# A decayed-attention and hard-swish MLP kernel: the first half tile's units given out more slowly, and the last tile's output units put in a row

## The chip, the cores and the metric

The kernel runs on one core of a Trainium2 chip. The metric is the device time of one execution in microseconds (us). The kernel before was run three times: 1083.11, 1084.06 and 1090.14 us, median 1084.06 us. One further execution was profiled; it is the one that the views below show.

## The reference

There are 8 batches of 8 heads with 576 rows of 64 elements, all in f32. The attention is causal, with a decay between a query and a key that is the difference of a running sum of log f. The result goes, with the heads of a row side by side, through a two-layer MLP.

```python
def _attn_ref(q, k, v, f):                     # (8, 8, 576, 64), f: (8, 8, 576)
    scores = np.matmul(q, k.transpose(0, 1, 3, 2)) / np.sqrt(D)
    cum = np.cumsum(np.log(np.clip(f, 0.0001, 1.0)), axis=-1)
    scores = np.where(causal, -1000000000.0, scores + cum[..., :, None] - cum[..., None, :])
    attn = np.exp(scores - np.max(scores, axis=-1, keepdims=True))
    attn = attn / (np.sum(attn, axis=-1, keepdims=True) + 1e-09)
    return np.matmul(attn, v)
def _moe_ref(x, w_in, w_out):                  # x (4608, 512), w_in (512, 2048), w_out (2048, 512)
    h = x @ w_in
    g = h * np.clip(h + 3.0, 0.0, 6.0) / 6.0
    return g @ w_out
```

## The kernel before, in words

**Numbers in two parts.** A product of f32 numbers is computed as three fp16 matmuls (high by high, high by low, low by high), or as one fp32r matmul plus one for the remainders. This is why each line of a product stands three times in the MLP (L781, L782, L783 and L834, L835, L836) and why the scores have a second matmul (L609 and L612). The weights arrive in a wide format, and are decoded and split while attention already runs; `w_step` gives that work out piece by piece, and DVE's share of the split is L295.

**The steps.** The outer loop (L974 to L1042) runs over the list `VH` (L97): four steps of kind A (the first 256 query rows of batch 0, two heads at a time), eight of kind B (the other rows of batch 0's heads) and 56 of kind F, a full head each, of batches 1 to 7. The steps are numbered 0 to 67. Step 12 is the first head of the second batch, step 13 its second head. Names such as `pn_13_0` hold the step and the half of the head.

**One full head.** SP loads q and k into `ST` (L412) and the decay rows into TK and TQ (L418, L420). POOL copies q and k into TQ and TK (L447, L448). SP copies these by DMA to the other half of the partitions, into T7 and T1 (L454, L455), and POOL subtracts to get the remainders (L456, L459). PE then computes the scores `pn` in two halves (L609, L612); DVE adds the mask and takes the row maxima (`pp`, L620; `nb`, L626), ACT takes the exponential (L632), ACT, DVE and POOL write the two fp16 parts into a `ring` buffer (L646, L649, L655), SP transposes each half by DMA into `pT` (L667, two transposes a head), and PE multiplies by v into `pav` (L692 to L697). After each second head, the pair's rows are normalised (L721 to L733) and transposed by SP into `xT` and `xS` (L748, L753), which are the MLP's input. There are three buffers each of TK, TQ and ST, two of T1 and T7, three rings. v of a batch is loaded into `vst` (L360, L361) and its largest element found by DVE (L366) and PE (`pt_v`, L184), for the scale of its fp16 parts.

**The MLP as units.** A tile is 512 rows of a batch; the 64 rows left over are done for two batches at a time (`moe_short`). `h_unit` computes 128 of the 2048 hidden columns for a tile: 12 matmuls into one bank, then ACT (L789), DVE (L792, tile `r`), ACT (L793) and DVE (L794) write the two parts of `gT`. `out_unit` computes the output of 128 rows: 48 matmuls into one bank `po`, an ACT copy into `o` (L840, pool of two buffers) and an output DMA. Batch 0's tile is two half tiles of 256 rows: the first can begin when the four A steps are done, the second when the B steps are. Both kinds take their banks from `mm_tile`: two banks of one pool in turn, and, where `three` is set, each third tile another bank. The first half tile has `three=False` throughout and so the two banks alone.

**When the units come.** They stand in a queue, and `fill(1)`, called eight times in a step, adds `rates[0]` to a credit and issues units while the credit is at least 1 (L941 to L951). An h unit of the half tile costs 1.05 credits, an output unit 7.6. `rates[0]` is set once a step (L991), from `F_RATE[0]` in all of batch 0, from `F_RATE[1]` in the second batch, and after that so that what is left is spread evenly over the heads. The first half tile enters the queue at step 5, as 16 h units and 2 output units, some 32 credits. The second half tile enters at step 13.

**What sets the order.** The calls above give a priority; the order of instructions on each engine is then written out when the program is built, by a scheduler that has a model of the durations. On the chip each engine runs its list in order. `behind(on)` (L762) tells the scheduler that an instruction is to be issued after the last one on the list `chain`. In the kernel before this holds for the h units of the last tile (batch 7) and of the last leftover rows; its four output units and the two half-width ones of the leftover rows (`po_3456_0`, `po_3456_256`) are free in their order.

Of the kernel before, what the change touches and what calls it, by code (L numbers as in the profile page):

```python
# [20 lines left out]
def kernel(  # L21
# [10 lines left out]
    nc = tc.nc  # L32
# [3 lines left out]
    B = vS.shape[0]  # L36
# [9 lines left out]
    NFC = DFF // P  # L46
# [35 lines left out]
    NQK, NL, NST = 3, 2, 3  # L82
    W_RATE = (8, 2, 4)
    H_COST = 1.05
    F_RATE = (0.6, 0.45)
    PIN = 0
    PIN0 = 1
    LOW_W = 0
# [45 lines left out]
    w2 = cpool.tile([P, NFC + AHEAD, 2, DM], F16, name="w2")  # L134
# [18 lines left out]
    SV, IV, UO, UX, A1 = 0, 8, 16, 24, 32  # L153
# [47 lines left out]
    def scol(c):  # L201
        return SC[:, c:c + 1]
# [339 lines left out]
    def scores(v):  # L542

        i, j = v % NQK, v % NL
        ph = p2.tile([P, 1600], F32, tag="PHL", name=f"pf_{v}")

        def group(dst, k0, q0, q1, m):
            ks = slice(k0, k0 + P)
            nc.tensor.matmul(dst, TK[i][0:97, ks], TQ[i][0:97, q0:q1], start=True, stop=False)
            nc.tensor.matmul(dst, T1[j][:, ks], T7[j][:, q0:q1], start=False, stop=(m == 0))  # L550
            if m:
                nc.tensor.matmul(
                    dst[:, 0:m], W[:m, 4 * P:], ident16[:m, :m], start=False, stop=True
                )

        pc = 0
        for parts_, exps in pieces(v):
            ps = ps_s.tile([P, 2, 512], F32, tag="S", name=f"ps_{v}_{pc}")
            for bk, o, k0, q0, w, m in parts_:
                group(ps[:, bk, o:o + w], k0, q0, q0 + w, m)  # L560
            for e, (o, w, nb) in enumerate(exps):
                dst = ph[:, o:o + w]
                if nb == 2:
                    src = ps[:, :, :w // 2]
                    dst = dst.rearrange("p (a b) -> p a b", a=2)
                else:
                    src = ps.rearrange("p a b -> p (a b)")[:, e * 512:e * 512 + w]
                nc.scalar.activation(dst, src, AF.Exp, bias=bias_p, scale=0.125)
                pc += 1
            yield  # L570
            yield ph
# [7 lines left out]
    for half in NAT:  # L579
        g = [0]  # L580
# [179 lines left out]
    chain = []  # L760

    def behind(on):  # L762
        return tc.issue_after(chain[-1]) if on and chain else nullcontext()

    def mm_tile(name, three):

        turn[0] += 1
        if three and turn[0] % 3 == 0:
            return ps_t.tile([P, TT], F32, tag="tr", name=name)
        return ps_m.tile([P, TT], F32, tag="mm", name=name)  # L770
# [56 lines left out]

    def out_unit(s, three, col, rows_, gs=None, cols=(0, DM)):
        g = gT if gs is None else gs
        c = slice(*cols)  # L830
        po = mm_tile(f"po_{rows_[0]}_{cols[0]}", three)[:, c]
        ts_ = slice(s * P, (s + 1) * P)
        for fc in range(NFC):
            nc.tensor.matmul(po, g[:, 0, fc, ts_], w2[:, fc, 0, c], start=(fc == 0), stop=False)  # L834
            nc.tensor.matmul(po, g[:, 0, fc, ts_], w2[:, fc, 1, c], start=False, stop=False)  # L835
            nc.tensor.matmul(po, g[:, 1, fc, ts_], w2[:, fc, 0, c], start=False, stop=(fc == NFC - 1))  # L836
            if fc % 2 and fc < NFC - 1:
                yield 2.0 - H_COST
        o = p2.tile([P, DM], F32, tag="o", name=f"o_{rows_[0]}_{cols[0]}")
        nc.scalar.activation(o[:, c], po, AF.Copy, scale=scol(col))  # L840
        w = P // len(rows_)
        for i, r0 in enumerate(rows_):
            nc.sync.dma_start(out[r0:r0 + w, c], o[i * w:(i + 1) * w, c])
        yield 2.0 - H_COST

    def moe_tile(t, c0=0, c1=TT):
        last = t == B - 1
        if last:
            gs = vst.bitcast(F16).rearrange("p c e -> p (c e)")[:, 0:2 * NFC * P]
            gs = gs.rearrange("p (a f t) -> p a f t", a=2, f=NFC)  # L850
        for fc in range(NFC):
            j, new = divmod(fc, NFC // NG)
            if new == 0 and c0 == 0:
                while j not in w_in_done:
                    next(w_in_q, None)
                moe_scale_in(t, j)
            yield from h_unit(t, fc, c0, c1)
            if last and new == 1:
                yield from h_short(t // 2, j, gs)
        if t == 0:  # L860
            for _ in wq:
                pass
        if c0 == 0:
            moe_scale_out(t)
        r0 = t * S + (64 if t else 0)
        for s in range(c0 // P, c1 // P):
            yield from out_unit(s, t > 0 or s * P >= QA, UO + t, [r0 + s * P])
        if last:
            for cols in ((0, DM // 2), (DM // 2, DM)):
                yield from out_unit(0, True, UX + t, [(t - 1) * S, t * S], gs, cols)  # L870

    def moe_short(u):
        for j in range(NG):
            yield from h_short(u, j, gT)
        a, b = 2 * u, 2 * u + 1
        yield from out_unit(0, True, UX + b, [b * S - 64] if a == 0 else [a * S, b * S])
# [55 lines left out]
    def even(h):  # L932

        heads = (1 - h) % H + 1
        return min(max((left[0] - RESERVE) / (8 * heads), 0.5), 1.25)
# [38 lines left out]
    for i, (kind, n) in enumerate(VH):  # L974
# [13 lines left out]
        if moved is not None:  # L988
            done(moved)
            moved = None  # L990
        rates[0] = F_RATE[0] if kind == "B" else F_RATE[b] if b < 2 else even(h)  # L991
        sg = rows(i) if kind == "F" else scores(i)
# [95 lines left out]
```

## Time and profile before

| | |
|---|---|
| median of three runs | 1084.06 us (1083.11 to 1090.14) |
| the profiled execution's own time | 1081.36 us |
| span in the profile | 1079.5 us |
| granted TensorE clock, mean | 0.983 |
| busy share of PE, DVE, ACT, POOL | 94%, 66%, 54%, 38% |
| PE busy between 310 and 1050 us | 736.79 of 740 us |
| PE busy between 130 and 310 us | 156.91 of 180 us |

PE is TensorE's matmuls, PEld its weight loads, DVE VectorE, ACT ScalarE, POOL GpSimd, SP SyncE, which issues the DMAs. The span counts from the first to the last recorded instruction; the profiled execution's own time is 1.86 us longer than its span and 2.7 us under the median of the three runs. Times in the views are us from the start of the span. In a row of a timeline, the numbers ahead are the start and the time of one instruction or of a group, and what stands in brackets at the end is how long the engine had been idle and what ended that. "issue" means that the profile shows nothing that was waited for.

### The profile page before, as it was taken

How to read it: one execution, taken by the hardware profiler on the slowest of the kernel's cores; microseconds unless marked ns; L12 is line 12 of the kernel's file. 1: busy time of each engine (PE TensorE's matmuls, PEld its weight loads, DVE VectorE, ACT ScalarE, POOL GpSimd, SP SyncE). 2: the span in 40 equal slices, each digit the busy share in tenths (PEclk: the TensorE clock that was granted, in tenths of full speed). 3: DMA queues.
4: the chain of work that ended last, by engine and by line, in shares of the span. 5: the costliest groups of instructions: out<-in, count | busy, mean ns of one | idle time of the engine just before them, and what ended most of it. 6: DMA issues, size and time to landing. Idle time of an engine off the chain costs nothing.

```text
span 1079.5 us, 21234 instructions
## 1 busy us (share of the span) xinstructions
PE 1016.3 (94%) x7698; PEld 608.5 (56%) x7698; DVE 714.6 (66%) x1903; ACT 587.5 (54%) x1190; POOL 407.8 (38%) x505
## 2 busy tenths in 40 slices
PE   2889987899989999999999999999999999999997
PEld 1557846765545665555555755555555755545545
DVE  6887968776986669865875668766865678505400
ACT  4787736664664456744654457555654566415400
POOL 7344434546534444543343345444434442100000
PEclk9989988989999999999999999999999999999999
DMA  8976326877767586577645666666565555400001
GB/s 250 287 215 198 111 60 127 147 173 161 147 139 149 118 160 119 115 141 143 145 90 123 127 150 132 128 136 162 99 118 124 96 108 87 91 30 1 1 3 47
DMA packets 259300, 133.79 MB, mean 124 GB/s; under 512 B 226964, under 2 KB 228812, under 8 KB 259196
## 3 DMA queue, kind: packets, MB, share of 16 engines
q1 hardware_dynamic: 259196, 132.44, 55.8%
q8 instruction: 61, 1.00, 0.4%
q14 instruction: 43, 0.35, 0.1%
HBM read 47.93 MB, written 9.73 MB: 53 GB/s over the span
## 4 chain that ended last, share of the span: by engine, by line
PE 66%; DVE 12%; issue 6%; DMA 6%; ACT 5%; POOL 3%; SPq 1%; ACTq 0%; POOLq 0%; DVEq 0%
PE po L834 10%; PE po L836 10%; PE po L835 10%; PE ph L781 7%; PE ph L783 6%; PE ph L782 6%; PE pn L609 3%; PE pn L612 3%; DMA vst<-in_vS_dram 2%; DVE pp L620 2%; ACT pp L632 2%; PE pav L703 2%; PE low L287 1%; DMA pT<-ring 1%; DVE gT L794 1%
## 5 line engine op out<-in xcount | busy, mean ns | idle before, releaser
L632 ACT ACTIVATE pp<-pp,nb 128x192 f32<-128x192 f32 x280 | 138.4, 552 | 148.8 <-DVE nb L626 143.7
L834 PE MATMUL po<-w,gT 128*128 128x512 f16 x560 | 210.2, 383 | 6.1 <-DVE r L792 4.7
L836 PE MATMUL po<-w,gT 128*128 128x512 f16 x560 | 209.7, 382 | 0.0
L835 PE MATMUL po<-w,gT 128*128 128x512 f16 x560 | 209.5, 382 | 0.0
L781 PE MATMUL ph<-xT,w 128*128 128x512 f16 (+1 forms) x576 | 201.8, 359 | 6.2 <-DVE r L792 6.2
L782 PE MATMUL ph<-xT,w 128*128 128x512 f16 (+1 forms) x576 | 200.9, 358 | 0.0
L783 PE MATMUL ph<-xT,w 128*128 128x512 f16 (+1 forms) x576 | 200.8, 358 | 0.0
L649 DVE TENSOR_TENSOR ring<-pp,ring 128x128 f16<-128x128 f32 (+2 forms) x216 | 138.9, 652 | 85.8 <-ACT ring L646 85.0
L620 DVE CUSTOM_DVE_ANT_0 pp<-pn,W 128x192 f32<-128x192 f32 x280 | 123.1, 481 | 34.9 <-PE pn L612 23.8
L447 POOL TENSOR_SCALAR TK<-ST 64x576 fp32r<-64x576 f32 (+1 forms) x68 | 50.8, 747 | 247.2 <-PE pn L609 172.5
L459 POOL TENSOR_TENSOR T<-ST,T 64x576 fp32r<-64x576 f32 (+1 forms) x68 | 101.4, 1492 | 88.8 <-DMA T<-TK 83.9
L609 PE MATMUL pn<-TK,TQ 68*128 68x192 f32 x336 | 125.5, 387 | 6.6 <-issue 5.5
L793 ACT CAST gT<-r 128x512 f16<-128x512 f32 (+1 forms) x144 | 81.7, 568 | 77.6 <-DVE r L792 77.3
L792 DVE SCALAR_TENSOR_TENSOR r<-r,ph 128x512 f32<-128x512 f32 (+1 forms) x144 | 88.9, 619 | 51.1 <-ACT r L789 50.7
L612 PE MATMUL pn<-T,T 128*128 128x192 f32 x336 | 114.6, 368 | 2.2 <-POOL T L459 2.2
L794 DVE TENSOR_TENSOR gT<-r,gT 128x512 f16<-128x512 f32 (+1 forms) x144 | 102.2, 714 | 19.4 <-ACT gT L793 18.2
L789 ACT ACTIVATE r<-ph,bias_r,SC 128x512 f32<-128x512 f32 (+1 forms) x144 | 103.9, 725 | 19.2 <-PE ph L783 14.1
L646 ACT CAST ring<-pp 128x192 f16<-128x192 f32 x280 | 113.8, 450 | 0.0
L456 POOL TENSOR_TENSOR T<-ST,TQ 64x576 fp32r<-64x576 f32 (+2 forms) x68 | 99.2, 1459 | 15.5 <-PE pn L612 5.8
L836 PEld LDWEIGHTS <-gT 128*128 128x128 f16 x560 | 55.0, 99 | 67.5 <-issue 7.4
L835 PEld LDWEIGHTS <-gT 128*128 128x128 f16 x560 | 55.0, 99 | 67.3 <-issue 11.3
L840 ACT ACTIVATE o<-po,SC 128x512 f32<-128x512 f32 (+1 forms) x37 | 24.7, 673 | 120.7 <-PE po L836 115.8
(154 smaller groups left out, 2026.4 us busy)
## 6 DMA issues: line engine op xcount, KB each, us to landing
ST<-in_qk_dram SPq DMA_DIRECT2D x64, 288.0 KB
T<-TK SPq DMA_DIRECT2D x64, 144.0 KB
out_dram<-o SPq DMA_DIRECT2D x33, 256.0 KB
ring<-in_w_out_dram SPq DMA_DIRECT2D x16, 512.0 KB
T<-TQ SPq DMA_DIRECT2D x56, 144.0 KB
vst<-in_vS_dram SPq DMA_DIRECT2D x7, 1040.0 KB
ring<-in_w_in_dram SPq DMA_DIRECT2D x9, 512.0 KB
w<-in_w_in_dram SPq DMA_DIRECT2D x7, 512.0 KB
```

The lines of the kernel that those rows point to most:

```text
L609: nc.tensor.matmul(dst, TQ[i][0:D + 4, qs], TK[i][0:D + 4, a:e], start=True, stop=False)
L612: nc.tensor.matmul(dst, T7[j][:, qs], T1[j][:, a:e], start=False, stop=True)
L620: nc.vector.tensor_tensor_reduce(pp[:r, w:w + kw], pn[:r, o:o + kw], W[:r, 4 * P + r - kw:4 * P + r], 1.0, -3.0e38, ALU.add, ALU.max, accu ...
L632: nc.scalar.activation(x_, x_, AF.Exp, bias=nb[:r, e0 + x:e0 + x + 1], scale=0.125)
L646: nc.scalar.copy(hl[:r, h0[c]:h0[c] + kw], pp[:r, at[c]:at[c] + kw])
L649: eng.tensor_tensor(hl[:r, a:a + c * P], pp[:r, at[c] + 64:at[c] + kw], hl[:r, h0[c] + 64:h0[c] + kw], op=ALU.subtract,)
L781: nc.tensor.matmul(ph, w1[0][:, cc, fs_], xh, start=(cc == 0), stop=False)
L782: nc.tensor.matmul(ph, w1[0][:, cc, fs_], xl, start=False, stop=False)
L783: d = nc.tensor.matmul(ph, w1[1][:, cc, fs_], xh, start=False, stop=(cc == NCC - 1))
L834: nc.tensor.matmul(po, g[:, 0, fc, ts_], w2[:, fc, 0, c], start=(fc == 0), stop=False)
L835: nc.tensor.matmul(po, g[:, 0, fc, ts_], w2[:, fc, 1, c], start=False, stop=False)
L836: nc.tensor.matmul(po, g[:, 1, fc, ts_], w2[:, fc, 0, c], start=False, stop=(fc == NFC - 1))
```

## The change

There are two edits. `F_RATE[0]` goes from 0.6 to 0.45, so the credits in batch 0 come more slowly. At 0.6, 32 credits take about 53 calls of `fill`, and the first half tile's units end at the start of step 12; at 0.45 they take about 71, and end in step 14, the third head of the second batch. And `out_unit` joins the chain: for the output scales of the last tile and of the last leftover rows, each unit's first matmul is issued after the last matmul of the unit before.

```diff
-    F_RATE = (0.6, 0.45)
+    F_RATE = (0.45, 0.45)
...
     def out_unit(s, three, col, rows_, gs=None, cols=(0, DM)):
         g = gT if gs is None else gs
+        last = col in (UO + B - 1, UX + B - 1)
...
         for fc in range(NFC):
-            nc.tensor.matmul(po, g[:, 0, fc, ts_], w2[:, fc, 0, c], start=(fc == 0), stop=False)
+            with behind(last and fc == 0):
+                nc.tensor.matmul(po, g[:, 0, fc, ts_], w2[:, fc, 0, c], start=(fc == 0), stop=False)
             nc.tensor.matmul(po, g[:, 0, fc, ts_], w2[:, fc, 1, c], start=False, stop=False)
-            nc.tensor.matmul(po, g[:, 1, fc, ts_], w2[:, fc, 0, c], start=False, stop=(fc == NFC - 1))
+            d = nc.tensor.matmul(
+                po, g[:, 1, fc, ts_], w2[:, fc, 0, c], start=False, stop=(fc == NFC - 1)
+            )
             if fc % 2 and fc < NFC - 1:
                 yield 2.0 - H_COST
+        if last:
+            chain.append(d.ins)
```

The PE lists of the two kernels hold the same instructions. They differ in order from row 276 to about step 28, and again in the last tile. Lines behind L829 move down with the added code: L834 to L836 become L836 to L838, the output DMA becomes L849.

**PE, the first scores of the second batch.** Before, both output units of the first half tile, 96 matmuls of 512 columns, stand between the scores of step 12 and those of step 13. In the changed list step 13's scores follow directly behind step 12's, and the two output units lie between step 13's scores and step 14's.

**DVE, the last h units of the first half tile.** `r_0_11` is the result of hidden column 11 of the first half tile, `mr_11` the row maxima that step 11's scores need, `vm1` the largest elements of the second batch's v in `vst`, and L295 splits weights. Before:

```order
L792 SCALAR_TENSOR_TENSOR r_0_11_0_1100<-r_0_11_0_1100,ph_0_11_0_1087 128x256
L794 TENSOR_TENSOR gT_116<-r_0_10_0_1058,gT_116 128x256
...
L502 TENSOR_SCALAR mr_11_1502<-ptm_11_1500 3x128
...
L792 SCALAR_TENSOR_TENSOR r_0_13_0_1168<-r_0_13_0_1168,ph_0_13_0_1155 128x256
L794 TENSOR_TENSOR gT_116<-r_0_12_0_1142,gT_116 128x256
L366 TENSOR_REDUCE vm1_1579<-vst_112 128x1 x2
```

Now:

```order
L792 SCALAR_TENSOR_TENSOR r_0_10_0_1115<-r_0_10_0_1115,ph_0_10_0_1102 128x256
L366 TENSOR_REDUCE vm1_1533<-vst_112 128x1 x2
L295 SCALAR_TENSOR_TENSOR w2_115<-w2_115,SC_121 128x512 x2
L502 TENSOR_SCALAR mr_11_1466<-ptm_11_1464 3x128
L295 SCALAR_TENSOR_TENSOR w2_115<-w2_115,SC_121 128x512
L794 TENSOR_TENSOR gT_116<-r_0_10_0_1115,gT_116 128x256
L792 SCALAR_TENSOR_TENSOR r_0_11_0_1142<-r_0_11_0_1142,ph_0_11_0_1129 128x256
```

What moved: the two reductions over `vst`, which wait for the load of v, stood behind `r_0_13`; they now stand ahead of `mr_11` and `r_0_11`.

**SP, the transposes and the T copies.** `L454` and `L455` copy TQ and TK of a step into T7 and T1; a transpose of a head's ring can only be issued when that head's softmax is done. In the regular case a step's two copies stand behind the second transpose of the head three steps earlier. Before, this is so except for steps 16, 19 and 20 among the first full heads, whose L455 stands behind a transpose of the head two steps earlier. Step 16's (buffer T10) stands there behind both transposes of head 13 and the first of head 14:

```order
L667 DMA_TRANSPOSE pT_13_1742<-ring2_126 128x13x128
L454 DMA T70_101<-TQ1_94 64x576
L748 DMA_TRANSPOSE xT0_117<-xhl_10_1641 128x4x128
L753 DMA_TRANSPOSE xS0_119<-xhl_10_1641 128x2x64
L667 DMA_TRANSPOSE pT_13_1742<-ring0_124 128x12x128
L667 DMA_TRANSPOSE pT_14_1880<-ring1_125 128x13x128
L455 DMA T10_99<-TK1_97 64x576
```

In the changed kernel steps 16, 19 and 20 are regular, and it is the copies of steps 22 and 23 that stand behind a transpose of head 20 and of head 21. Step 22's:

```order
L667 DMA_TRANSPOSE pT_19_2648<-ring0_124 128x12x128
L849 DMA out_0_dram<-o_256_0_2866 128x512
L667 DMA_TRANSPOSE pT_20_2791<-ring1_125 128x13x128
L667 DMA_TRANSPOSE pT_20_2791<-ring2_126 128x12x128
L412 DMA ST0_103<-in_qk_dram 128x576
L420 DMA TQ2_95<-decay_dram 2x576
L454 DMA T70_101<-TQ1_94 64x576
L455 DMA T10_99<-TK1_97 64x576
```

What moved: of three late copies in the list before, two remain, and they lie three to six heads later.

**PE, the end.** `po_4480_0` is the last output unit of the last tile, `po_3456_0` and `po_3456_256` are the two half-width units. Before, the three run mixed and their last matmuls are:

```order
L834 MATMUL po_3456_256_12528<-w2_115,vst_112 128x256
L835 LDWEIGHTS vst_112
L835 MATMUL po_3456_256_12528<-w2_115,vst_112 128x256
L836 LDWEIGHTS vst_112
L836 MATMUL po_3456_0_12475<-w2_115,vst_112 128x256
...
L836 MATMUL po_4480_0_12423<-w2_115,gT_116 128x512
L834 LDWEIGHTS gT_116
L834 MATMUL po_4480_0_12423<-w2_115,gT_116 128x512
```

Now each unit's 48 matmuls stand together, `po_4096_0`, `po_4224_0`, `po_4352_0`, `po_4480_0`, `po_3456_0`, `po_3456_256`, and the list ends so:

```order
L838 MATMUL po_3456_256_12528<-w2_115,vst_112 128x256
L836 LDWEIGHTS vst_112
L836 MATMUL po_3456_256_12528<-w2_115,vst_112 128x256
L837 LDWEIGHTS vst_112
L837 MATMUL po_3456_256_12528<-w2_115,vst_112 128x256
```

What moved: three units whose matmuls stood mixed to the end now stand one after the other, a half-width one last.

## The prediction

> **What bounds the kernel now.** I read the page first, then the table of busy time by stage, then the waits of the stages in which the bound is not held, and at last single rows.
>
> ```profile
> span 1079.5 us, 21234 instructions
> ...
> PE 1016.3 (94%) x7698; PEld 608.5 (56%) x7698; DVE 714.6 (66%) x1903; ACT 587.5 (54%) x1190; POOL 407.8 (38%) x505
> ```
>
> PE is busy for 1016.3 of 1079.5 us. No matmul is added or removed, so the change can only gain where PE stands still or runs at a reduced clock. The table by stage shows where that is (columns: the stage, its length, busy time of PE, PEld, DVE, ACT and POOL, granted clock, DMA share, GB/s).
>
> ```profile
> 108.00:130.00 22.00, 21.67 (x183) 18.63 (x182) 19.86 (x62) 17.79 (x35) 7.72 (x9) 1.00 0.42 118
> 130.00:163.00 33.00, 28.34 (x144) 15.69 (x144) 22.33 (x53) 13.72 (x27) 12.60 (x11) 0.90 0.24 61
> 163.00:190.00 27.00, 21.47 (x209) 17.81 (x208) 23.12 (x77) 17.71 (x42) 13.43 (x15) 0.87 0.70 132
> 190.00:240.00 50.00, 43.90 (x448) 33.42 (x447) 38.12 (x131) 32.38 (x78) 24.38 (x23) 0.93 0.80 159
> 240.00:285.00 45.00, 41.32 (x294) 23.46 (x293) 32.54 (x99) 25.93 (x57) 25.89 (x32) 0.92 0.76 159
> 285.00:310.00 25.00, 21.88 (x178) 12.37 (x177) 20.90 (x42) 14.71 (x28) 11.20 (x15) 1.00 0.74 164
> 310.00:1050.00 740.00, 736.79 (x5668) 414.34 (x5667) 471.73 (x1193) 387.96 (x769) 257.29 (x331) 1.00 0.53 107
> 1050.00:1079.50 29.50, 21.70 (x148) 14.18 (x145) 0.00 (x0) 3.48 (x6) 0.00 (x0) 0.95 0.14 46
> ```
>
> From 310 to 1050 PE idles 3.2 of 740 us at full clock: nothing to gain. From 130 to 285, the seam between batch 0 and the full heads, it idles 4.66 + 5.53 + 6.10 + 3.68 = 20.0 us, and the clock takes at most 0.10 x 33 + 0.13 x 27 + 0.07 x 50 + 0.08 x 45 = 13.9 us more. From 1050 on it idles 7.8 us. Those two stages are where the two edits act. In the seam the engines waited thus (columns: us in total, times, longest):
>
> ```profile
> POOL T L459 <- DMA T<-TK: 32.1, 10, 6.0
> ...
> PE pn L609 <- issue: 5.5, 2, 4.5
> ...
> PE po L834 <- DVE r L792: 4.7, 1, 4.7
> ```
>
> POOL's second remainder waits for SP's copy of TK in every head, and the scores wait for POOL. PE itself has one long wait for DVE and two whose end the profile doesn't explain.
>
> **Part one, the end: the chain.** ACT's rows of the end, then PE's wait before the last units:
>
> ```profile
> 1050.74 1.27 ACT L840 ACTIVATE o<-po,SC 128x512 f32<-128x512 f32 x2 [28.93 <-PE po L836]
> ...
> 1072.56 1.05 ACT L840 ACTIVATE o<-po,SC 128x512 f32<-128x512 f32 x2 [16.75 <-PE po L836]
> 1075.39 0.47 ACT L840 ACTIVATE o<-po,SC 128x256 f32<-128x256 f32 x1 [1.77 <-DMA out_dram<-o]
> ```
>
> ```profile
> PE po L834 <- ACT o L840: 0.8, 1, 0.8
> ```
>
> The mixed units finish together. At 1072.56 ACT finds two of them and copies both; the third then waits 1.77 us for an output DMA to free one of the two `o` buffers, and is copied from 1075.39 to 1075.86. From there to the span's end are 1079.5 - 1075.86 = 3.64 us. Chained, the last unit is a half-width one, and when it ends the unit before it was copied long ago: between the two ACT rows of full banks, less the wait of 0.8, PE does the last three units, 48 matmuls of 512 columns and 96 of 256, in 1072.56 - 1050.74 - 0.8 = 21.0 us, so a half-width one takes a quarter of that, 5.2 us, more than any copy and DMA wait here. Only one copy of 0.47 us is left behind PE, and both buffers are free. The end comes at 1072.56 + 0.47 + 3.64 = 1076.67 us, 2.8 us earlier. The 0.8 us wait goes too: it arose when two banks were full at once at 1050.74, and in a row one bank is emptied while the next fills. Together -3.6 us; at the least -2.0, if a new wait of the size of 0.8 stands at each of two unit borders. The chain adds no wait for another engine: each unit is behind its predecessor on PE alone, which runs in order anyhow, and no other work is left that could have stood between.
>
> **Part two, the seam: the lower rate.** What is moved: 1.2 credits a step from steps 5 to 11, some 8 credits, come later. They lie on PE up to 130 us, where the first row of the table has PE busy 21.67 of 22 us: PE is the bound there, so what leaves that stage shortens it, and what joins the seam lengthens it by the same. The effect is in the idle time.
>
> Three of DVE's rows from 121 to 139 us:
>
> ```profile
> 121.53 0.40 DVE L792 SCALAR_TENSOR_TENSOR r<-r,ph 128x256 f32<-128x256 f32 x1
> ...
> 130.01 2.88 DVE L366 TENSOR_REDUCE vm<-vst 128x1 f32<-128x1536 f32 x2 [1.91 <-issue]
> ...
> 138.50 0.41 DVE L792 SCALAR_TENSOR_TENSOR r<-r,ph 128x256 f32<-128x256 f32 x1
> ```
>
> *The old wait.* DVE stood idle 1.91 us before the reduction of v, worked on it 2.88 us and on weights after that, and the r at 138.50 (column 14) came late; PE's 4.7 us wait for r is this one. The reductions now stand earlier, so this wait goes: -4.7 us.
>
> *A new wait.* The pair now stands ahead of the r of 121.53 (column 11) and of the row maxima for step 11's scores. If v lands no earlier than before, the pair ends near 130.01 + 2.88 = 132.9, and that r is up to 11.4 us late. PE has two banks for these units, so it can still do the 12th column and step 10's attention and then stops. The r is late against a later unit too, since the units come more thinly: I put the wait at 4 us, with 0 (v lands in time) and 9 us (11.4 less two units of 12 matmuls of 256 columns, each 21.0 / 192 = 0.11 us by the end's sum) as the ends. The clock of the stage, 0.90 with one such gap, I leave as it is. Net of old and new: -0.7 us, between -4.7 and +4.3.
>
> *The late copies.* PE's rows at the first score of steps 12, 13, 14 and 24, and POOL's T rows that follow the late copies of steps 16, 19 and 20:
>
> ```profile
> 132.38 0.36 PE L609 MATMUL pn<-TK,TQ 68*128 68x192 f32 x1
> ...
> 164.89 0.44 PE L609 MATMUL pn<-TK,TQ 68*128 68x192 f32 x1
> ...
> 171.38 0.34 PE L609 MATMUL pn<-TK,TQ 68*128 68x192 f32 x1
> ...
> 284.71 0.44 PE L609 MATMUL pn<-TK,TQ 68*128 68x192 f32 x1
> ```
>
> ```profile
> 191.54 1.46 POOL L459 TENSOR_TENSOR T<-ST,T 64x576 fp32r<-64x576 f32 x1 [2.46 <-DMA T<-TK]
> ...
> 229.16 1.40 POOL L459 TENSOR_TENSOR T<-ST,T 64x576 fp32r<-64x576 f32 x1 [4.62 <-DMA T<-TK]
> ...
> 237.86 1.41 POOL L459 TENSOR_TENSOR T<-ST,T 64x576 fp32r<-64x576 f32 x1 [5.95 <-DMA T<-TK]
> ```
>
> Before, step 13's scores came 32.5 us after step 12's, because the two output units lay between; then ten steps took 113.3 us, 11.3 each. The break empties the softmax, and when it is over, steps 13 and 14 come 6.5 us apart and the rest must wait for the first of them to come through DVE, ACT and SP. Between 163 and 190 this shows twice: a gap whose end the chain of waits calls
>
> ```profile
> 175.44 4.44 issue
> ```
>
> and step 16's copy, which stands on SP behind the transposes of heads 13 and 14, so that POOL's T is ready only at 193.0. That stage loses 5.53 us idle and 0.13 x 27 = 3.5 of clock, 9.0 in all. In the new order step 13's scores directly follow step 12's, so that the softmax runs during the output units, and step 16's copies are regular. The restart isn't gone entirely: steps 12 and 13 now come as closely as 13 and 14 did. I count three quarters: -6.8 us, with 0 and -9.0 as ends. Steps 19 and 20 become regular too, but steps 22 and 23 take over their kind of delay, a pair again; 190 to 285 lost 6.10 + 3.68 idle and 7.1 of clock, 16.9 us, and I count no gain there, with +3 (two waits more like POOL's 2.46, shorter ones) and -9.6 (the pair costs what 240 to 285 lost, 7.3) as ends.
>
> What covers the copies that cost nothing: a regular copy is followed by some 8.7 us of PE work per step (113.3 us less the 9.0 + 16.9 lost, over 10). If that is missing, each late one costs up to its 5.95 us.
>
> A rule that speaks against this edit: the Trainium skill, page "TensorE: Matmul & The Clock Gate", section "HAM oscillation — how this bites in real kernels", says that PE gaps above some 3.4 us drop the clock to half for a window. By it the new wait of 4 us, an estimate of mine, would bring 1.7 us of clock loss by itself, and thinner filling would cost more than its idle time; with the old 4.7 us gap gone the same rule gives that back. The traces agree in that 285 to 310 idles 3.1 us in small pieces at clock 1.00, while 163 to 190, with its 4.44 us gap, has 0.87. By the rule the sum below would differ by no more than 1.7 us either way.
>
> **Sum.** -3.6 (end) - 0.7 (DVE) - 6.8 (restart and step 16) + 0 (pair) = -11.1 us. The profiled execution's own 1081.36 us (span 1079.5 and 1.86 around it) becomes 1070.3; it lies 2.7 under the median of the runs, 1084.06, which becomes 1073.0.
>
> **The rivals.**
>
> *The whole seam closes.* PE's work would then cover the copies of steps 22 and 23 almost alone, and the pair costs 7.3 in place of 16.9. For it: without the break, the head chain is some 30 us further when the units come. Against it: POOL waits for that copy ten times in the seam, in steps that are regular as well. -3.6 - 0.7 - 9.0 - 9.6 = -22.9: 1061 us.
>
> *Only the end gains.* The idle time of the seam moves to steps 22 and 23 and keeps its size, since the loads, softmax and copies of the first full heads need their time whatever PE has to do. For it: the same units, the same heads, and PE idle in each of the four rows of the seam, with all other engines under 90%. Against it: after 285 the same heads run at full clock with little idle. -3.6: 1080.4 us.
>
> *Slower, by the load of v.* The reductions over v stand ahead of r and of the row maxima on DVE. If v lands as late as before, the pair ends at 132.9, PE stops for 9 us, and with it the scores of step 11 and all full heads come later. The stage then loses 9 and, as 130 to 163 did with one such gap, 3.3 of clock, and nothing else is gained: -3.6 + 12.3 = +8.7, 1092.8 us. For it: DVE was idle for exactly this pair, 1.91 us, before. Against it: the units before column 11 come later at the lower rate, so that the load has more time. It decides from the point where the wait exceeds some 4 us net of what the old one gave.
>
> That the change doesn't do what it says is left out: the lists show both moves.
>
> **How the numbers follow.** My forecast, 1067 to 1080, has 0.50; the whole seam 0.18; only the end 0.20; slower by the load 0.12. The range reaches from 1062, the whole seam with about a microsecond left, to 1087, where the slow case begins; it holds the ends of the single costs as long as not all of them fall on one side. Outside are most of the slow case and a third of the fast one, less than 0.2. One per cent, about what a measurement of this kernel can tell from no change, is 10.8 us: below 1073.2 or above 1094.9. Half of the forecast and the whole seam are faster by that: 0.25 + 0.18 = 0.43. The slow case passes 1094.9 half the time, 0.06. The rest, 0.51, is within.
>
> **What would show it.** The end: ACT's last L840 copy starts within 0.2 us of PE's last matmul, and no wait for an output DMA stands before it. DVE: no wait of PE for r of 4 us around step 12; instead one before column 13, with L366 just ahead on DVE; if that is over 8 us, the slow rival is right. The seam: the first scores of steps 12 and 13 a few us apart, idle time of 163 to 190 halved and its clock near 1; idle time now around steps 22 and 23. If the four rows of the seam keep their 20 us of idle time, only the end has gained. My forecast is wrong if the seam's idle time and clock loss, 33.9 us before, come out above 31 or below 20.

## The result, and the profile after

The changed kernel takes 1072.71 us, median of four runs (1071.82 to 1075.81); the kernel before, beside it, 1084.59 us. The ratio is 0.9886, 95% interval 0.9846 to 0.9927. Two further comparisons, made with the experiments below, give 0.9911 (0.9881 to 0.9941) and 0.9893 (0.9871 to 0.9915). The forecast was 1073.0 us.

The page of the changed kernel has the same PE work in a shorter span:

```profile
span 1074.0 us, 21231 instructions
...
PE 1017.6 (95%) x7698; PEld 610.8 (57%) x7698; DVE 724.9 (67%) x1903; ACT 588.6 (55%) x1190; POOL 408.7 (38%) x505
```

This profiled execution took 1075.81 us, the longest of the four, while that of the kernel before lay under its median. So the two pages are 5.5 us apart and the medians 11.9. Where a stage is judged below, the changed kernel's later profiles are read too. The table by stage of the changed kernel, with the columns and stages of the prediction's (stage, length, PE, PEld, DVE, ACT, POOL, granted clock, DMA share, GB/s):

```profile
108.00:130.00 22.00, 22.00 (x163) 18.38 (x162) 15.69 (x55) 13.10 (x28) 5.03 (x5) 0.84 0.44 124
130.00:163.00 33.00, 28.78 (x170) 20.10 (x170) 30.50 (x73) 20.91 (x40) 16.21 (x14) 0.84 0.30 72
163.00:190.00 27.00, 26.40 (x247) 19.21 (x246) 21.09 (x72) 16.17 (x37) 11.17 (x14) 1.00 0.64 147
190.00:240.00 50.00, 42.90 (x435) 32.15 (x435) 49.77 (x149) 34.80 (x82) 28.80 (x28) 0.97 0.82 169
240.00:285.00 45.00, 41.33 (x335) 23.81 (x332) 32.66 (x85) 27.61 (x58) 27.55 (x34) 0.92 0.92 190
285.00:310.00 25.00, 23.73 (x157) 13.27 (x155) 23.08 (x56) 15.59 (x31) 8.50 (x12) 1.00 0.46 94
310.00:1050.00 740.00, 735.61 (x5658) 413.54 (x5657) 466.70 (x1176) 386.77 (x764) 257.37 (x329) 1.00 0.53 108
1050.00:1074.00 24.00, 19.76 (x139) 13.41 (x137) 0.00 (x0) 1.64 (x3) 0.00 (x0) 1.00 0.11 33
```

From 163 to 190 us PE now stands still for 0.6 us, and the clock is full; it was 5.53 us and 0.87. From 108 to 163 the clock is worse than before, 0.84 in both rows where it was 1.00 and 0.90. From 190 to 285 little has changed: 7.1 + 3.7 us idle, against 6.1 + 3.7.

PE's first scores of steps 12 and 13, 32.5 us apart before, are now 6.1 us apart:

```profile
145.17 0.51 PE L609 MATMUL pn<-TK,TQ 68*128 68x192 f32 x1
```

```profile
151.28 0.26 PE L609 MATMUL pn<-TK,TQ 68*128 68x192 f32 x1
```

This holds for the first of the two halves of step 13's scores alone. Its second half, which the prediction took to follow as well, comes 19 us later, behind most of the matmuls of the two output units:

```profile
170.28 0.50 PE L609 MATMUL pn<-TK,TQ 68*128 68x320 f32 x1
```

Of PE's waits from 108 to 310 us the "issue" of 4.5 us is gone (one of 2.4 us remains), while one of 4.2 us for an h unit has come:

```profile
PE ph L781 <- DVE r L792: 7.3, 5, 4.2
PE pn L612 <- POOL T L459: 4.2, 2, 3.5
PE pn L609 <- issue: 2.4, 1, 2.4
```

At the end, ACT's rows show what the chain did:

```profile
1064.61 0.47 ACT L846 ACTIVATE o<-po,SC 128x256 f32<-128x256 f32 x1 [4.55 <-PE po L838]
1069.85 0.47 ACT L846 ACTIVATE o<-po,SC 128x256 f32<-128x256 f32 x1 [4.77 <-PE po L838]
```

The half-width units end 5.24 us apart (5.2 was forecast), and the last copy waits for PE alone: it starts 0.09 us behind the end of PE's last matmul, at 1069.76. From its start to the end of the span are 1074.0 - 1069.85 = 4.15 us; before, 1079.5 - 1072.56 = 6.94 us passed from the copies' first start.

### The profile page after: what moved, and what is told of

Same layout as the page of the kernel before. It is cut to its first block, busy times and chain, and to the rows that moved or that the text cites. A ratio compares the mean times of both kernels' runs of the same rounds, so it can differ in the third digit from the quotient of the medians.

```text
span 1074.0 us, 21231 instructions
## 1 busy us (share of the span) xinstructions
PE 1017.6 (95%) x7698; PEld 610.8 (57%) x7698; DVE 724.9 (67%) x1903; ACT 588.6 (55%) x1190; POOL 408.7 (38%) x505
## 4 chain that ended last, share of the span: by engine, by line
PE 72%; DVE 12%; ACT 4%; DMA 4%; issue 4%; POOL 2%; SPq 1%; ACTq 0%; DVEq 0%; POOLq 0%
PE po L836 11%; PE po L837 11%; PE po L838 11%; PE ph L781 8%; PE ph L783 8%; PE ph L782 8%; PE pn L612 3%; PE pn L609 3%; DVE pp L620 2%; ACT pp L632 2%; PE pav L703 2%; DVE gT L794 1%; DVE ring L649 1%; DVE r L792 1%; DMA vst<-in_vS_dram 1%
## 5 line engine op out<-in xcount | busy, mean ns | idle before, releaser
L781 PE MATMUL ph<-xT,w 128*128 128x512 f16 (+1 forms) x576 | 204.5, 363 | 11.0 <-DVE r L792 11.0
L836 PE MATMUL po<-w,gT 128*128 128x512 f16 x560 | 209.2, 381 | 0.7 <-ACT gT L824 0.7
L838 PE MATMUL po<-w,gT 128*128 128x512 f16 x560 | 208.1, 380 | 0.0
L782 PE MATMUL ph<-xT,w 128*128 128x512 f16 (+1 forms) x576 | 204.0, 362 | 0.0
L783 PE MATMUL ph<-xT,w 128*128 128x512 f16 (+1 forms) x576 | 203.7, 362 | 0.0
L794 DVE TENSOR_TENSOR gT<-r,gT 128x512 f16<-128x512 f32 (+1 forms) x144 | 108.1, 753 | 20.9 <-ACT gT L793 19.5
L838 PEld LDWEIGHTS <-gT 128*128 128x128 f16 x560 | 54.5, 98 | 66.5 <-issue 6.3
L655 POOL TENSOR_TENSOR ring<-pp,ring 128x128 f16<-128x128 f32 x96 | 60.4, 630 | 82.6 <-ACT ring L646 32.0
L782 PEld LDWEIGHTS <-w 128*128 128x128 f16 x576 | 57.2, 99 | 58.6 <-issue 16.4
```

What stands on the lines that cost most here:

```text
L781: nc.tensor.matmul(ph, w1[0][:, cc, fs_], xh, start=(cc == 0), stop=False)
L782: nc.tensor.matmul(ph, w1[0][:, cc, fs_], xl, start=False, stop=False)
L783: d = nc.tensor.matmul(ph, w1[1][:, cc, fs_], xh, start=False, stop=(cc == NCC - 1))
L794: nc.vector.tensor_tensor(gT[:, 1, fc, c0:c1], r, gT[:, 0, fc, c0:c1], op=ALU.subtract)
L838: d = nc.tensor.matmul(po, g[:, 1, fc, ts_], w2[:, fc, 0, c], start=False, stop=(fc == NFC - 1))
```

## The experiments

All of these kernels compute the whole result. The first four ran at one time, the next four later on the same chip, the last four on another chip, each group with the kernel before beside it. Ratios are to that. They are not exactly those of the two medians; differences in us are worked out from the ratios.

### The chain alone

```diff
-    F_RATE = (0.45, 0.45)
+    F_RATE = (0.6, 0.45)
```

> The rate of batch 0 back at 0.6, the output units of the last tile chained as in the changed kernel; up to the last tile the lists are those of the kernel before. Own theory (the end gives 3.6 us, the seam the rest): 3.6 us under the kernel before, about 1080.5 us; ACT's last copy follows PE's last matmul within 0.2 us. Rival (the chain carries nearly all of the gain, since mixed units cost more than the end shows): about 1073 us. Rival (the end is hidden by the last output DMA): no change, 1084.5 us.

1080.08 us beside 1081.4, ratio 0.9976 (0.9951 to 1.0): -2.6 us. The own theory's 3.6 lies in the interval, nothing like the whole gain does. No change lies at its edge, so it is the rows of the end, more than the time, that show the gain. The last copy of ACT, and the end of the span:

```profile
span 1079.3 us, 21234 instructions
```

```profile
1075.21 0.47 ACT L846 ACTIVATE o<-po,SC 128x256 f32<-128x256 f32 x1 [4.77 <-PE po L838]
```

The end is 4.1 us behind the copy's start, as in the changed kernel.

### The rate alone

```diff
-    F_RATE = (0.6, 0.45)
+    F_RATE = (0.45, 0.45)
```

in the kernel before, without the other edit.

> Only the rate, 0.45, with the last tile's output units free as before. Own theory: the seam's gain alone, 7.5 to 8.5 us under the kernel before, about 1076.5 us, so that this run's gain and that of the chain alone add up to the whole 11.9 us. Rival (the two edits do not add up, one covers the other): gains that sum to clearly more or less than 12 us. The seam's idle time is that of the changed kernel, the end's 7 us between PE's last matmul and the end of the span as before.

1075.59 us, ratio 0.9938 (0.9914 to 0.9961): -6.7 us. With the chain's 2.6 that makes 9.3 us; the whole change measured between 9.6 and 12.4 us (0.0089 to 0.0114 of 1084). The edits add up as far as the intervals tell. The rate leaves the end as it was:

```profile
1070.02 1.05 ACT L840 ACTIVATE o<-po,SC 128x512 f32<-128x512 f32 x2 [16.81 <-PE po L836]
1072.84 0.47 ACT L840 ACTIVATE o<-po,SC 128x256 f32<-128x256 f32 x1 [1.77 <-DMA out_dram<-o]
```

### The load of v one head earlier

```diff
-        if b + 1 < B and h == 6:
+        if b + 1 < B and h == (5 if b == 0 else 6):
             load_v(b + 1)
```

in the changed kernel.

> The changed kernel with the load of the second batch's v issued one head earlier, so that it should have landed before DVE reaches the reduction. The lists change otherwise too: of the late copies in the seam only step 19's and 27's are left, in place of steps 22 and 23. Own theory (DVE's wait for v holds up r and costs PE the 4.2 us wait and the half clock after it): the wait goes, 4 to 6 us under the changed kernel, 1067 to 1069 us, up to 9 us more if the late copies of steps 22 and 23 cost what I took them to. Rival (the wait is covered elsewhere: what PE wins there it waits for the heads later): no change, 1072.7 us.

1074.75 us, ratio 0.9928 (0.99 to 0.9955). PE's wait of some 4 us for DVE's r is gone, the longest wait for an r from 110 to 310 us is now 1.0 us. But the time isn't under that of the changed kernel, as the rival had it. The stage after the wait:

```profile
108.00:130.00 22.00, 21.66 (x159) 18.79 (x160) 18.81 (x56) 11.90 (x26) 7.07 (x7) 0.84 0.47 130
130.00:163.00 33.00, 31.32 (x205) 23.12 (x203) 32.80 (x80) 24.99 (x49) 19.80 (x17) 0.90 0.33 87
```

PE's idle time from 130 to 163 falls from 4.2 us (2.1 and 2.3 in the changed kernel's later profiles) to 1.7, and yet the clock is at 0.84 and 0.90. Here the lists differ in other places as well. So the run shows that this edit, with the wait gone, doesn't shorten the kernel; it doesn't show what the wait alone was worth, or what takes its place.

### The copies into T7 and T1 earlier

```diff
     def rests(v):
...
-        nc.sync.dma_start(T7[j].bitcast(F32)[0:D, 0:nq], TQ[i].bitcast(F32)[0:D, 0:nq])
-        nc.sync.dma_start(T1[j].bitcast(F32)[D:, 0:nk], TK[i].bitcast(F32)[0:D, 0:nk])
+        with tc.high_priority(offset=100):
+            nc.sync.dma_start(T7[j].bitcast(F32)[0:D, 0:nq], TQ[i].bitcast(F32)[0:D, 0:nq])
+            nc.sync.dma_start(T1[j].bitcast(F32)[D:, 0:nk], TK[i].bitcast(F32)[0:D, 0:nk])
```

in the kernel before.

> The kernel before, rate 0.6 and no chain, but the copies into T7 and T1 are issued with a higher priority. On SP steps 16, 19 and 20 then become regular (only step 14's, 28's and 33's copies stand behind a transpose of the head two steps earlier), while the two output units still lie between the scores of steps 12 and 13. It tells late copies from the break. If the late copies cost the seam its time: half of the 9.0 us of step 16 and most of the 16.9 us of steps 19 and 20 go, 12 to 20 us under the kernel before, 1064 to 1072 us. If the break does: little, 0 to 4 us, 1080 to 1084 us.

1083.45 us, ratio 1.0021 (1.0003 to 1.0038): no gain. Two of its stages:

```profile
163.00:190.00 27.00, 21.70 (x169) 17.11 (x168) 21.80 (x68) 13.47 (x31) 13.92 (x14) 0.87 0.47 104
190.00:240.00 50.00, 44.78 (x455) 33.34 (x453) 45.56 (x136) 36.21 (x86) 26.28 (x26) 0.97 0.85 167
```

With steps 16, 19 and 20 regular on SP and the break between steps 12 and 13 still there, 163 to 190 loses 5.3 us and a clock of 0.87, as before. So the late copy of step 16 isn't needed for that loss. The longest wait of PE there is now another one, 3.6 us for DVE (`xf`, L728 in this kernel).

### The changed kernel again

> The changed kernel again, timed beside the other kernels of this group on the same chip. Own theory: end 3.6 us and seam 5 to 7 us under the kernel before, ratio 0.990 to 0.992. Rival (the first comparison was near the truth with its 0.9886): 12 us under.

1072.46 us beside 1082.52, ratio 0.9911.

### The output units held back

Rate 0.6, the chain, and the first half tile's output units kept in the queue until step 13 (`now[0]` is set to the step at the head of the loop):

```diff
         r0 = t * S + (64 if t else 0)
+        while t == 0 and c0 == 0 and now[0] < 13:
+            yield None
...
                 r = next(units[0], 0)
+            if r is None:
+                break
```

> The chain, and the rate at 0.6, but the two output units of the first half tile are kept in the queue until step 13. Up to step 12's scores PE's and DVE's lists are those of the kernel before (v is reduced behind column 13's r); then step 13's scores come after only part of po_0_0, and those of steps 14 and 15 soon after po_128_0 begins. But six copies in the seam (steps 18, 19, 20, 24, 27, 29) stand behind a transpose of the head two steps earlier. If the break between steps 12 and 13 costs the time (own theory): the 7 us lost from 163 to 190 go without the thinner filling before 130 us; with the end's 3.6 about 10 us under the kernel before, level with the changed kernel or up to 3 us under it. If it is the late copies: 3 to 10 us above the changed kernel. If it is the thin filling as such: level with the chain alone, 3.6 us under the kernel before.

1079.91 us, ratio 0.9969 (0.9949 to 0.9988), level with the chain alone, which is what was expected if the thin filling as such gains. (The profiled execution, 1075.89 us, lies 4.0 under that median.) The break is gone, and with it the loss where the theory put it, but the next stage loses more than was gained:

```profile
163.00:190.00 27.00, 24.80 (x282) 19.06 (x280) 25.19 (x81) 18.78 (x44) 15.41 (x18) 1.00 0.85 177
190.00:240.00 50.00, 33.74 (x357) 27.45 (x354) 41.51 (x125) 29.75 (x71) 23.81 (x26) 0.86 0.79 158
240.00:285.00 45.00, 45.00 (x327) 24.26 (x326) 31.56 (x86) 24.61 (x49) 19.20 (x25) 1.00 0.81 174
```

From 190 to 240 PE idles 16.3 us, and the clock takes up to 0.14 x 50 = 7.0 more. The longest waits there, of PE:

```profile
PE pav L692 <- DMA pT<-ring: 7.9, 3, 6.0
PE ph L782 <- DVE r L793: 6.2, 3, 4.7
```

PE waits for a head's transposes and for DVE; from 240 to 285 it doesn't idle at all. Work that could have filled the gap stands behind it on PE's list.

### The rate 0.55

```diff
-    F_RATE = (0.45, 0.45)
+    F_RATE = (0.55, 0.45)
```

> The chain, and the rate 0.55. The reductions over v stand ahead of column 11's r, as in the changed kernel, but both output units still lie between the scores of steps 12 and 13, as before. Own theory (the break costs the time): the seam gains nothing, only the end's 3.6 us, so 6 us above the changed kernel. Rival (any thinner filling up to step 12 gains): between 0.6 and 0.45, some 6 to 8 us under the kernel before.

1073.72 us, ratio 0.9917 (0.9886 to 0.9948). The own theory missed: the break is still there, and the gain nearly that of the changed kernel.

```profile
130.00:163.00 33.00, 33.00 (x203) 21.23 (x202) 22.31 (x59) 18.72 (x37) 10.82 (x11) 1.00 0.27 67
163.00:190.00 27.00, 19.19 (x176) 15.75 (x175) 22.70 (x70) 13.80 (x33) 12.15 (x12) 0.75 0.59 128
```

The stage behind the break loses more than before: 7.8 us idle and a clock of 0.75 from 163 to 190. Its longest wait is one for SP's transposes into `xT`, the input of the second half tile's h units, not for a score (PE's longest waits of the stage, then DVE's reductions over v):

```profile
PE ph L781 <- DMA xT<-xhl: 4.8, 1, 4.8
PE pn L609 <- issue: 2.1, 1, 2.1
```

```profile
121.31 2.88 DVE L366 TENSOR_REDUCE vm<-vst 128x1 f32<-128x1536 f32 x2 [1.19 <-DMA vst<-in_vS_dram]
```

But 130 to 163 loses nothing where the kernel before lost 4.66 us idle and 0.10 of the clock. The reductions over v stand ahead of column 11 here too, but v is there 8 us earlier than in the changed kernel's first profile, and PE found no wait for an r. And 190 to 285 loses 10.6 us, idle time and clock together, where the kernel before lost 16.9.

### The rate 0.35

```diff
-    F_RATE = (0.45, 0.45)
+    F_RATE = (0.35, 0.45)
```

> The chain, and the rate 0.35. The scores of steps 12, 13, 14 and 15 come close together on PE, with po_0_0 ahead of step 12's and po_128_0 behind step 13's: no break. Late copies are those of steps 19, 20 and 23. Own theory: the 163 to 190 loss goes as in the changed kernel, but more idle time and half clock before 130 us, 2 to 4 us more there; level with the changed kernel to 3 us above it. Rival (the thinner the better, as the seam gets more work to hide its waits): 2 to 5 us under the changed kernel.

1070.48 us, ratio 0.9894 (0.9871 to 0.9917), level with the changed kernel, as the own theory had it; though not for the reason given. From 60 to 130 us its two profiles (the second is of the repeat below) lost 6.9 and 8.7 us, idle time and clock together, against 11.4, 9.4 and 10.5 in the changed kernel's three; and from 163 to 190 they idled 5.0 and 5.6, where the changed kernel idles 0.6 to 1.6.

### Held units and early copies

The edit that holds the output units back and the one that issues the copies early, together, at the rate 0.6 and with the chain.

> The chain, rate 0.6, the two output units kept in the queue until step 13, and the T7 and T1 copies issued with a higher priority. Step 13's scores follow soon after step 12's, and of the late copies in the seam only step 24's is left. The run with the held units alone lost little from 163 to 190 us and some 22 us from 190 to 240, of matmul work that could have been done. If three late copies in a row (steps 18, 19, 20) cost that: the 190 to 240 loss falls to the 6 to 8 us of the other kernels, and the time is 10 us or more under the held units alone, 12 to 16 us under the kernel before. If it is the heads running ahead of what DVE and the transposes can follow: the loss of 15 us or more stays, 3 to 5 us under the kernel before.

1082.2 us, ratio 1.0008 (0.9993 to 1.0024). The 190 to 240 loss stays without the late copies:

```profile
163.00:190.00 27.00, 23.06 (x189) 15.52 (x187) 16.39 (x62) 14.22 (x35) 13.00 (x12) 0.87 0.67 127
190.00:240.00 50.00, 36.90 (x411) 32.79 (x409) 45.91 (x142) 32.40 (x77) 28.71 (x30) 0.87 0.89 178
```

13.1 us idle. So it is not three late copies in a row; that the heads run ahead of what follows them fits, but wasn't tested by itself. And from 163 to 190 this kernel loses 3.9 us idle and 0.13 of the clock, 7.5 us, though step 13's first scores come only 11.5 us after step 12's (149.63 and 138.17 us): a stage without the break can lose nearly as much as one with it.

### The rate 0.35 with early copies, and two kernels again

> The chain, rate 0.35, copies with a higher priority: no late copy in the seam, and step 13's scores behind both output units, with step 12's directly ahead of them; the h units are thin. If the late copies matter once the seam is filled thinly: 3 to 6 us under the rate of 0.35 alone. If not, no difference from it, or the break between steps 12 and 13 takes back up to 5 us.

1073.12 us, ratio 0.9926 (0.9902 to 0.995): no gain from regular copies in a thin filling either. The break between steps 12 and 13 that the expectation has in this list isn't in the trace: step 13's first scores come at 146.15 us, 6.5 us after step 12's at 139.70.

> The chain and the rate 0.35 again, beside the changed kernel on the same chip. Expected: ratio to the kernel before between 0.988 and 0.991, 0 to 3 us under the changed kernel; whether it is faster than that by more than the measurement tells is open.

> The changed kernel a third time, for the comparison on the same chip with the rate of 0.35. Expected: ratio to the kernel before 0.989 to 0.992.

1072.62 us (0.9906, 0.9876 to 0.9937) for the rate of 0.35 and 1070.6 us (0.9893) for the changed kernel. Over both groups neither is faster than the other.

## Why the prediction was right, point by point

Idle time of PE plus (1 - clock) x length, from the table by stage of each kernel, in us. The first column is the mean of the kernel before and the chain alone, which have the same list up to the last tile, the second the mean of the three profiles of the changed kernel and that of the rate alone:

| stage | rate 0.6 | rate 0.45 | difference | forecast |
|---|---|---|---|---|
| 60 to 108 | 6.4 | 7.9 | +1.5 | none |
| 108 to 163 | 8.3 | 9.2 | +0.9 | -0.7 |
| 163 to 190 | 9.0 | 0.9 | -8.1 | -6.8 |
| 190 to 285 | 16.8 | 16.3 | -0.5 | 0 |
| 285 to 310 | 2.3 | 1.5 | -0.8 | none |
| sum | 42.8 | 35.8 | -7.0 | -7.5 |

The two profiles of the first column lost 41.9 and 43.7 us in all, the four of the second between 32.6 and 38.6. The seam from 130 to 285, whose 33.9 us the prediction wanted between 20 and 31, lost 26.0, 22.9 and 21.2 us in the three profiles of the changed kernel. That the sum came so near is luck in part: up to 163 us the change gave 3.1 us less than forecast, behind that 2.6 more.

**The end, -3.6.** Right, by its own steps. In the four traces of the rate 0.45 with or without the chain, the time from the first of the last copies to the end of the span is 4.1 us chained and 6.9 free, -2.8 as worked out, and the 0.8 us wait of PE appears in no chained trace. By its run times, the chain alone measured -2.6 with an interval from -5.3 to 0.

**The old wait and the new one.** Right in kind and size. DVE waited for v, and PE for DVE (DVE's rows, then PE's, of the changed kernel):

```profile
129.49 2.88 DVE L366 TENSOR_REDUCE vm<-vst 128x1 f32<-128x1536 f32 x2 [1.70 <-DMA vst<-in_vS_dram]
...
136.37 0.40 DVE L792 SCALAR_TENSOR_TENSOR r<-r,ph 128x256 f32<-128x256 f32 x1
```

```profile
136.82 0.37 PE L781 MATMUL ph<-xT,w 128*128 128x256 f16 x1 [4.22 <-DVE r L792]
```

I had put 4 us, of 0 to 9; it is 4.2 here, 5.0 and 3.4 in the later profiles of the changed kernel and 3.7 with the rate alone. The step that failed lies before it. I took PE for the bound up to 130 us, so that what leaves that stage shortens it and nothing else. But in three of these four traces PE now waits 1.87 us for DVE's `xf` between 101 and 108 us, where the two profiles of the rate 0.6 in the table have none and one of 0.8, and the clock is at half for 6.8 us behind it (the rows are in the last section). From 108 to 130 the four lose 2.6 to 3.5 us, in three of them mostly or in good part by this clock; before it was 0.3.

The slower rival had the right mechanism and missed its size, since column 11 comes later at the lower rate: DVE writes the r of column 10 at 127.36 us, where it was 120.23, while the reductions over v begin at about the same time, 129.49 and 130.01. Its price was too high by the prediction's own terms as well. It counts the new wait of 9 us with 3.3 of clock, but doesn't take off the old wait of 4.7 and its clock, which go by the same move; with them it comes to 0.7 us over the kernel before, not 8.7.

**The restart and step 16, -6.8.** The size was right, -8.1, and one half of its reason fell. With the break, 163 to 190 lost 9.0 us (before, and the chain), 8.8 (early copies) and 14.6 (rate 0.55). Where step 13's first scores follow 6 to 13 us behind step 12's it lost 0.5 to 1.6 (the rate 0.45), 0.6 (v early), 2.2 (units held back), 3.7 to 5.6 (the three profiles of the rate 0.35) and 7.5 (held units and early copies). But PE's longest wait in the stage is a different one each time: 4.5 us that the profile doesn't explain before, 3.6 for `xf` with the early copies, 4.8 for `xT` at the rate 0.55. That the break stands behind all three is argued, not shown. And the late copy of step 16, which I named beside the break, isn't needed for the loss: the early copies removed it and the stage lost as much; POOL's T for it, ready at 193.0 us, lay behind the stage anyhow. And the step from this stage to the whole time isn't general: with the units held back at the rate of 0.6, the stage lost 2.2 us, and 190 to 240 then 23.3 in place of some 9. Rate 0.55 gained without mending the break.

**The pair of late copies, 0.** Right as a sum, and wrong in what it was thought to be. I took 16.9 us from 190 to 285 for the price of the late copies of steps 19 and 20, and let 22 and 23 inherit it. Kernels that have no such copies lose nearly as much there (13.5 us with early copies at rate 0.6, 15.1 with early copies at 0.35), and their time isn't lower. By the first of these, some 3.4 of the 16.9 us could have been the copies' own. Nor does POOL's wait for such a copy tell a late one: by the line that I read as a wait in every head, POOL waited ten times, for fifteen of these subtractions between 130 and 310 us.

In the changed kernel one of the two copies that I had inheriting the delay does stop PE, where I had said that idle time would be (SP's issue of step 22's copy, POOL's subtraction, PE's second matmul of these scores):

```profile
252.81 0.60 SPq L455 DMA_DIRECT2D T<-TK  x1
```

```profile
257.00 1.54 POOL L459 TENSOR_TENSOR T<-ST,T 64x576 fp32r<-64x576 f32 x1
```

```profile
258.59 0.53 PE L612 MATMUL pn<-T,T 128*128 128x192 f32 x1 [3.47 <-POOL T L459]
```

The wait is 3.4 to 3.5 us in all four traces of the rate 0.45; before, PE's longest wait for POOL's T was 1.4 us. In the first profile it makes nearly all of the 3.7 us idle from 240 to 285. Yet with v loaded earlier step 22's copy is regular and this wait is gone, and the stage still loses 6.2 us in place of 7.3, in other waits. (By the same measure the copies of steps 15 and 27 are late in the changed list too; besides the wait for step 22's, PE has one of 0.7 us for POOL's T from 108 to 310.)

**The rivals.** The whole seam didn't close, and the gain was not the end's alone: the rate by itself measured -6.7 with an interval from -9.3 to -4.2. The slow case didn't occur.

**What stays open.** Why every kernel with a rate of 0.55 or less gains some 5 to 10 us in the seam (its ratio less the chain's), with its break or without, while the three others with 0.6 (early copies, held units, both) gain less than 1 us there, whatever they mend. The traces tell where each loses (0.6 with the break: 130 to 190; 0.6 without: 190 to 240), not a single wait that the rate removes. A mean over few profiles can't settle it: executions of one and the same kernel differed by up to 10 us (1066.4 to 1076.2 us for the changed kernel).

## What to carry to other kernels

When units that end together share an engine and a pool of buffers for their last copies, put them in a row with the shortest last; what that gives can be worked out to a few tenths from the rows of the end. In a stage in which several chains wait in turn, the stage that a stall is taken from says little about the whole: cost what is late next, and try the edit alone, since here three reasoned mends (v earlier, copies earlier, units held back) removed the waits that they were meant for and gave nothing. Read a gain of ten microseconds from medians and intervals, and use profiles of several executions to place it.

## What the runs showed of the hardware that was not expected

Short gaps of PE can cost more than themselves. In the first profile of the changed kernel PE idles once for 1.87 us just ahead of a stage in which it is busy throughout (PE's timeline, then the table by stage):

```profile
106.72 1.58 PE L703 MATMUL pav<-v,pf 128*128 128x96 f32 x12 [1.87 <-DVE xf L727]
```

```profile
108.30:115.10 6.80, 6.80 (x33) 4.82 (x33) 5.41 (x23) 4.09 (x9) 1.58 (x1) 0.50 0.46 135
```

For 6.8 us after that the granted clock is 0.50, which costs 3.4 us, nearly twice the gap. The Trainium skill, page "TensorE: Matmul & The Clock Gate", section "HAM oscillation — how this bites in real kernels", gives gaps above some 3.4 us as the ones to avoid; here 1.87 us was enough. With the rate alone and in the third profile of the changed kernel the same gap of 1.87 us was followed by 6.8 us at half clock too. In its second profile the same wait was 0.97 us, and the stage behind it ran at full clock:

```profile
104.39 1.58 PE L703 MATMUL pav<-v,pf 128*128 128x96 f32 x12 [0.97 <-DVE xf L727]
```

```profile
108.00:130.00 22.00, 19.11 (x164) 16.72 (x162) 18.49 (x52) 14.01 (x28) 7.40 (x8) 1.00 0.41 117
```

So the same list loses the clock in one execution and not in the next. The length of a gap doesn't settle it either: in the first profile PE idles 2.42 us a little later, and the clock behind that stays full:

```profile
200.96 0.33 PE L609 MATMUL pn<-TK,TQ 68*128 68x192 f32 x1 [2.42 <-issue]
```

```profile
201.00:217.00 16.00, 12.56 (x139) 10.93 (x140) 16.00 (x41) 11.46 (x27) 8.29 (x10) 1.00 0.75 147
```

By the prediction's reading of that rule the clock could move the sum by 1.7 us either way; between the three profiles of the changed kernel the clock loss from 60 to 310 us is 17.7, 10.5 and 11.6 us. That spread, 7.2 us, is as large as what the rate alone was worth, 6.7 us.
